# Eight units in the first routing group, and two sigmoid groups in another place

## The chip, the core and the metric

One core of a Trainium2 chip. The metric is the device time of one execution in microseconds; the figure for a kernel is the median of its runs.

## What is computed

Two stages, the second on the output of the first. Stage one is a gated linear attention with a running state (batch 4, 8 heads, 768 steps, head size 40), stage two a mixture of eight experts with two experts per token (3072 tokens of 320 features, hidden size 1024).

```python
for t in range(S):                       # attention
    m_new = np.maximum(f_gate[:, :, t] + m, i_gate[:, :, t])
    f_stab = np.exp(f_gate[:, :, t] + m - m_new); i_stab = np.exp(i_gate[:, :, t] - m_new)
    C = f_stab * C + i_stab * outer(vt, kt);  n = f_stab * n + i_stab * kt
    denom = np.maximum(np.abs(n . qt), 1.0)
    y[:, :, t] = sigmoid(o_gate[:, :, t]) * (C @ qt) / denom

logits = x @ w_gate                      # routing
noisy = logits + np.log1p(np.exp(x @ w_noise)) * noise
top2 = the two largest of noisy;  top2_w = softmax over these two
for e in range(8):                       # experts
    h = np.maximum(x[tokens of e] @ w1[e], 0.0)
    out[tokens of e] += top2_w * (h @ w2[e])
```

## The kernel before

**Attention loop.** The recurrence is worked in chunks of 64 steps. A unit is one chunk of one pair of batches, 128 tokens; there are 24 units. The loop `while i < NU - LEAD` runs iterations 0 to 21, one per unit; units 22 and 23 are written out behind it. The order of instructions on each engine is written by hand: the program text is the order of each engine's queue. Iteration i works on several units at once: DVE scales the keys of unit i+1 (`k_part`, L367), PE updates the state (`c_part`, L387) and ACT copies it into the next unit's operand (L390); PE forms the outputs of unit i (`o_part`, L396); `e_part` makes the decays of unit i+2 in two halves, each a PE matmul (L336) into one PSUM bank and an ACT exponential out of it (L339); DVE normalizes (`f_part`, L401 to L407) and POOL multiplies by the sigmoid of the output gate (L408); DVE multiplies scores by decays for unit i+1 (`p_part`, L373, or L377 in halves); PE makes router logits of unit i-2 (`l_part`, L439), transposes the rows of unit i-1 (`t_part`, L419) and makes scores of unit i+2 (`s_part`, L359). Loads of unit i+3 are issued by SP and POOL at the top of the iteration (`load_unit`), where POOL or SP also stores finished rows to DRAM (`keep_rows`).

**Sigmoids.** ScalarE keeps one table set with exponential and logarithm; a sigmoid is three ACT steps in place (`sig_part`, L345): exponential of -x, logarithm of one plus that, exponential of its negative. The steps of unit i+1 stand in iteration i, the first ahead of `o_part`, the other two at its end; iterations 0 and 1 differ.

**Routing.** Six groups of four units (`GROUPS`). When the logits of a group's last unit are there, a generator `g_part(g)` is put into a list, and `fill` deals out its small DVE steps: up to 0.2 (in the program's own units of about a microsecond, 0.19 for most steps) behind `k_part`, 0.15 twice within `f_part`, and the rest of 1.6 at the iteration's end. The generator makes the noisy logits (three ACT steps are asked for in between, L719), the two largest and their indices (L569, L572), the weights (L575, L602 to L605), a running count of tokens per expert (rank matmuls `r_part`, L448 to L450), and from each token's rank one-hot tables OA (L649, L652) and OB (L655), steps marked "long", which only the fill at the iteration's end takes. A burst (`b_part`, L459) multiplies the tables of four units and adds to TBL, the list of tokens per expert and place; `done` counts the units in it. Tables are double buffered.

**What waits for the table.** Expert 0's rows are gathered (POOL, indirect DMA, L803) in three parts: when 12 units are done (`begun`, at the top of an iteration, two tiles, a third in the next), when 20 are done, and when all are. Behind the loop PE transposes the gathered rows (L833) and begins with expert 0 (`mm1`, L1031). The second part is gathered in the stretch of 72 matmuls that finish the first part of expert 0 (L1154); its transposes stand in the last third of these. There `advance` deals out the remaining routing. From then on the experts follow one another, with PE's order fixed throughout. POOL also makes the low parts of the first expert's weights, one piece (L147) at the end of iterations 11, 13, 17, 19, 20 and 21.

Of the kernel before, what the change touches and what calls it, by code (L numbers as in the profile page):

```python
# [10 lines left out]
HF = mybir.dt.float16  # L11
# [3 lines left out]
OP = mybir.AluOpType  # L15
# [3 lines left out]
NE, F, DM = 8, 1024, 320  # L19
# [8 lines left out]
TC = BLK // 128  # L28
# [5 lines left out]
FIT = 2048  # L34
FF = 1024
NM = 768
GROUPS = tuple((u, 4) for u in range(0, 24, 4))
GOF = {u: g for g, (u0, n) in enumerate(GROUPS) for u in range(u0, u0 + n)}
NB = 4

EF, LONG = 2, 3
NR = NE - EF
# [25 lines left out]
def build(ctx, tc, qk, vk, og, fi, noise, wgn, w1, w2, cst, ce, out):  # L68
    nc = tc.nc
    V, A, P, T, SP = nc.vector, nc.scalar, nc.gpsimd, nc.tensor, nc.sync  # L70
# [14 lines left out]
    spot = keep.tile([128, 128, 2], HF, name="spot")  # L85
    cols = keep.tile([128, NE * TC, 2], HF, name="cols")
    sgn = keep.tile([128, 2 * NU], HF, name="sgn")
# [47 lines left out]
    def piece_w1(j):  # L135
        k, p = j // 2, j % 2 if j < 4 else 1
        SP.dma_start(RAW1[64 * p:64 * p + 64, k], w1[0, 64 * j:64 * j + 64])
# [203 lines left out]
    def sig_part(u, ps_=(0, 1, 2)):  # L341

        g = SG[u % 4]
        for p in ps_:
            A.activation(g, g, (AF.Exp, AF.Ln, AF.Exp)[p], bias=float(p == 1), scale=(-1.0, 1.0, -1.0)[p])  # L345
# [64 lines left out]
    def keep_rows(u):  # L410
        (P if u < XV - 1 else SP).dma_start(XD[128 * u:128 * u + 128, 0:DM], XR[u])
# [86 lines left out]
    def decode(a, b, more=True):  # L498
        run(decode_steps(a, b, more))
# [10 lines left out]
    def lc_part(i, t, w):  # L510
        u = i - 2
        if 0 <= u < NU:
            g = GOF[u]
            c = u - GROUPS[g][0]
            if c == 0:
                LG[g] = rt.tile([128, NB, 16], F32, name="lg")
            A.activation(LG[g][:, c, :], t[:, LGC:LGC + 16], AF.Copy)
# [6 lines left out]
    anew = {}  # L524
    for nb in sorted({n for _, n in GROUPS}):
        anew[nb] = rt.tile([128, NE, nb + 1], BF, name=f"anew_{nb}", bufs=1)
        P.memset(anew[nb], 1.0)
        P.memset(anew[nb][:, :, 0], 0.0)
    bursts, done, acts, lag = [], [0], [], [1, 1]
    OBT = [rt.tile([128, 4, 128, 2], HF, name=f"ob{i}", bufs=1) for i in range(2)]  # L530
    OAT = [rt.tile([128, 4, NE * TC, 2], HF, name=f"oa{i}", bufs=1) for i in range(2)]

    def g_part(g):

        u0, nb = GROUPS[g]
        lg = LG[g][:, 0:nb]
        f = lambda a: a.rearrange("p u e -> p (u e)")
        fe = lambda a: a.rearrange("p e u -> p (e u)")
        sm = lambda name, shape, dt=F32: rt.tile(shape, dt, name=f"{name}_{nb}", bufs=1)
# [93 lines left out]
        ai = sm("ai", [128, 2 * nb], I32)  # L633
        V.tensor_scalar(ai, f(r), 7, None, op0=OP.arith_shift_right)
        yield
        n = 2 * nb
        assert n == 8
        bi = sm("bi", [128, n], HF)
        V.scalar_tensor_tensor(bi, ai, -128.0, f(r), op0=OP.mult, op1=OP.add)
        yield  # L640
        ah = sm("ah", [128, n], HF)
        V.tensor_copy(ah, ai)
        while done[0] < u0 - 4:
            yield "wait"
        OB, OA = OBT[g % 2], OAT[g % 2]
        C = NE * TC
        yield "long"
        two = lambda a, c: a.rearrange("p (a b) -> p a b", b=2)[:, :, None, :].to_broadcast([128, 4, c, 2])
        V.tensor_tensor(OA, cols[:, None].to_broadcast([128, 4, C, 2]), two(ah, C), op=OP.is_equal)  # L649
        yield 0.3  # L650
        yield "long"
        V.tensor_mul(OA, OA, two(sgn[:, 2 * u0:2 * u0 + n], C))  # L652
        yield 0.3
        yield "long"
        V.tensor_tensor(OB, spot[:, None].to_broadcast([128, 4, 128, 2]), two(bi, 128), op=OP.is_equal)  # L655
        yield 0.6
        bursts.append(([OB[:, j // 2, :, j % 2] for j in range(n)], [OA[:, j // 2, :, j % 2] for j in range(n)], unit[0] + lag[1]))
        if u0 + nb == NU:
            V.tensor_add(rk[:, 0:1], rk[:, 0:1], bump[0])
            yield  # L660
# [37 lines left out]
    spent, long = [0.0], set()  # L698
# [48 lines left out]
    def route(i):  # L747
        if 2 <= i <= NU + 1 and sum(GROUPS[GOF[i - 2]]) == i - 1:
            routing.append(g_part(GOF[i - 2]))
# [91 lines left out]
    unit = [0]  # L841
    clear = zeros()
    pre1 = first_w1()
    i = 0
    while i < NU - LEAD:
        unit[0] = i
        spent[0] = 0.0
        if 1 <= i and i + 3 < NU:
            load_unit(i + 3, "kv")
        if i:  # L850
            keep_rows(i - 1)
        if 1 <= i and i + 3 < NU:
            load_unit(i + 3, "g")
        if i % 2 == 0 and i and i // 2 + 2 < 2 * GB:
            gate_move(i // 2 + 2, (P, P) if i < XV else (SP, SP))

        if i in W1LD:
            piece_w1(W1LD.index(i))
        if i == W2AT:
            early_w2(0, 4)  # L860
        if i == 4:
            SP.dma_start(cs[:, C_TRI:], cst[:, C_TRI:])
        if i == 5:
            SP.dma_start(nzt, noise)
        while sent:
            SP.dma_start(*sent.pop())
        if not begun and done[0] >= E0U[0]:
            decode(0, E0S[1] // 128, 128 * E0U[0] > FIT)
            begun = 1
        if begun and late < len(tiles(0, 0)):  # L870
            gather(0, 0, tiles(0, 0)[late:late + 2])
            late += 2
            begun = 2
        if i == 6:
            constants()
            A.activation(tri, cs[:, C_TRI:C_TRI + 128], AF.Copy)
            A.activation(ones, cs[:, C_ONE:C_ONE + 128], AF.Copy)
            A.activation(sgn, cs[:, C_SGN:C_SGN + 2 * NU], AF.Copy)
        if i in (6, 7):
            n = slice(64 * (i - 6), 64 * (i - 6) + 64)  # L880
            A.activation(spot[:, n], cs[:, C_N:C_N + 128][:, n, None].to_broadcast([128, 64, 2]), AF.Copy)
        if i == 7:
            A.activation(cols, cs[:, C_COL:C_COL + NE * TC, None].to_broadcast([128, NE * TC, 2]), AF.Copy)
        asked = len(acts)
        k_part(i + 1)
        fill(0.2, False)
        s_room(i + 2)
        c_part(i)
        if i:
            sig_part(i + 1, (0,))  # L890
        o_room(i)
        o_part(i)
        e_part(i + LEAD, (0,))
        act(asked)
        if i == 0:
            sig_part(0)
        f_part(i, lambda: fill(0.15, False))
        p_part(i + 1)
        t = l_part(i)
        w = r_part(t)  # L900
        b = None if w else b_part(t)
        if i:
            t_part(i - 1)
            tc_part(i - 1)
        lc_part(i, t, w)
        bc_part(t, b)
        if i < 2:
            s_part(i + 2)
            e_part(i + LEAD, (1,))
            sig_part(i + 1, (1, 2) if i else (0, 1, 2))  # L910
        else:
            e_part(i + LEAD, (1,))
            s_part(i + 2)
            act()
            sig_part(i + 1, (1, 2))
        route(i)
        fill((SHARE if i < NU - 3 else 0.6) - spent[0])
        if i in W1AT:
            next(pre1)
        if i < 6:  # L920
            gates_on(GATES[i + 1])
        if 6 <= i < 13:
            P.memset(XG[:, i - 6], 0.0)
        i += 1
# [8 lines left out]
    u = NU - 2  # L933
# [19 lines left out]
    u = NU - 1  # L953
# [197 lines left out]
    for k, (l, r) in enumerate(((HH, W2H), (HLO, W2H), (HH, W2L))):  # L1151
        for n in range(24):
            t, j = divmod(n, 8)
# [261 lines left out]
```

## Time and profile before

| | us |
|---|---|
| median of three runs | 514.81 |
| lowest and highest run | 512.7, 516.75 |
| span of the profiled execution | 512.4 |
| PE busy in it | 497.5 (97%) |
| DVE, ACT, POOL busy | 331.3, 245.7, 231.1 |

The time of the profiled execution is given by its span, from the first instruction to the last; the runs' times are those of other executions. In the rows further down, times are microseconds from the span's start. PE is the matmul engine, PEld its weight loads, DVE the vector engine, ACT the scalar engine, POOL GpSimd, and SPq the queue of SyncE. L373 is line 373 of the kernel before. A bracket at the end of a timeline row is the engine's idle time ahead of the instruction and what ended it.

### The profile page before, as it was taken

What the parts mean: (1) busy time and instruction counts of PE and PEld (TensorE: products, weight loads), DVE (VectorE), ACT (ScalarE), POOL (GpSimd) and SP (SyncE); (2) the same over time, 40 slices, a digit from 0 to 9 for tenths busy, and PEclk for the clock granted to TensorE, in tenths of its full rate; (3) what the DMA queues carried; (4) which work ended last, traced back from release to release, by engine and by line L of the source; (5) the groups of instructions that cost most, each with busy time, mean ns of one, the idle gap of its engine ahead of it and who ended that gap; (6) DMA issues with size and microseconds to landing.
All of it is one profiled execution on the core that took longest, in us unless ns stands there. A gap on an engine that the chain in (4) does not pass through costs nothing.

```text
span 512.4 us, 13150 instructions
## 1 busy us (share of the span) xinstructions
PE 497.5 (97%) x5043; PEld 472.3 (92%) x5043; DVE 331.3 (65%) x935; ACT 245.7 (48%) x584; POOL 231.1 (45%) x303
## 2 busy tenths in 40 slices
PE   8899999998999999999999999999999999999995
PEld 4698888887999988999999999999999999999994
DVE  8868889889787586754853675375448347555410
ACT  7768888898623355423531543154235315514300
POOL 9736666265113876156135605531561354151033
PEclk9969999999999999999999999999999999999998
DMA  6888787877767465296159417723941682372033
GB/s 168 237 224 259 211 245 207 228 209 230 260 217 234 108 98 180 46 242 157 30 100 271 104 28 195 171 79 68 278 90 39 162 203 80 65 169 26 2 36 45
DMA packets 51493, 76.89 MB, mean 150 GB/s; under 512 B 10825, under 2 KB 41808, under 8 KB 51392
## 3 DMA queue, kind: packets, MB, share of 16 engines
q1 hardware_dynamic: 38576, 50.16, 33.7%
q0 software_dynamic: 12848, 25.82, 24.0%
q8 instruction: 42, 0.69, 0.6%
q14 instruction: 27, 0.22, 0.1%
HBM read 52.10 MB, written 17.32 MB: 135 GB/s over the span
## 4 chain that ended last, share of the span: by engine, by line
PE 83%; DVE 8%; DMA 4%; ACT 2%; issue 1%; POOL 1%; SPq 1%; POOLq 0%; DVEq 0%
PE s L1031 25%; PE e L1031 12%; PE o L1066 5%; PE o L1065 5%; PE o L1064 5%; PE st L1066 5%; PE st L1065 5%; PE st L1064 5%; PE o L396 3%; DVE p L373 2%; PE e L336 2%; PE s L359 1%; PE s L1154 1%; PE xt L439 1%; PE st L387 1%; DVE kd L367 1%
## 5 line engine op out<-in xcount | busy, mean ns | idle before, releaser
L1087 POOL DMA_INDIRECT y_out<-y,tok x53 | 87.2, 1646 | 178.6 <-DVE y L1077 177.5
L1044 ACT ACTIVATE hx<-s 128x384 fp32r<-128x384 f32 (+5 forms) x91 | 43.5, 478 | 72.7 <-PE s L1031 67.9
L1031 PE MATMUL s<-xh,w1h 128*128 128x384 f32 (+6 forms) x273 | 76.0, 336 | 0.0
L803 POOL DMA_INDIRECT xg<-rows,tok x53 | 56.3, 1062 | 35.7 <-issue 13.7
L1047 DVE SCALAR_TENSOR_TENSOR hx<-s,hx 128x384 fp32r<-128x384 f32 (+3 forms) x91 | 48.1, 528 | 34.2 <-ACT hx L1044 34.0
L1031 PE MATMUL s<-xh,w1l 128*128 128x384 f32 (+6 forms) x273 | 61.9, 334 | 0.0
L1066 PE MATMUL o<-w2h,hx 128*128 128x320 f32 x184 | 56.9, 309 | 0.0
L1064 PE MATMUL o<-w2h,hx 128*128 128x320 f32 x184 | 56.8, 309 | 0.0
L1065 PE MATMUL o<-w2l,hx 128*128 128x320 f32 x184 | 56.8, 309 | 0.0
L1066 PE MATMUL st<-w2h,hx 128*128 128x320 f32 x176 | 54.4, 309 | 0.0
L1064 PE MATMUL st<-w2h,hx 128*128 128x320 f32 x176 | 54.4, 309 | 0.0
L1065 PE MATMUL st<-w2l,hx 128*128 128x320 f32 x176 | 54.3, 309 | 0.0
L1031 PEld LDWEIGHTS s<-xh,w1h 128*128 128x128 f32 x273 | 48.8, 188 | 1.3 <-ACT xh L835 0.3
L1031 PEld LDWEIGHTS s<-xh,w1l 128*128 128x128 f32 x273 | 47.8, 188 | 1.1 <-DVE xh L837 0.2
L1031 PE MATMUL s<-xl,w1h 128*128 128x384 f32 (+6 forms) x182 | 46.0, 334 | 0.0
L1044 ACT ACTIVATE hx<-e 128x384 fp32r<-128x384 f32 (+5 forms) x45 | 21.7, 482 | 48.9 <-PE e L1031 36.2
L1077 DVE TENSOR_SCALAR y<-o,gw 128x320 f32<-128x320 f32 x23 | 12.7, 550 | 45.8 <-PE o L1066 45.8
L1077 DVE TENSOR_SCALAR y<-st,gw 128x320 f32<-128x320 f32 x22 | 12.1, 551 | 43.3 <-PE st L1066 43.3
L1031 PE MATMUL e<-xh,w1h 128*128 128x384 f32 (+6 forms) x135 | 38.4, 338 | 0.0
L408 POOL TENSOR_TENSOR xr<-tm,vk 128x320 f32<-128x320 f32 x24 | 20.9, 871 | 35.3 <-ACT w L339 10.4
L345 ACT ACTIVATE vk<-vk 128x320 f32<-128x320 f32 x72 | 33.8, 471 | 2.8 <-DMA vk<-og_in 1.9
L1064 PEld LDWEIGHTS o<-w2h,hx 128*128 128x128 f32 x184 | 34.5, 188 | 0.0
(247 smaller groups left out, 1242.1 us busy)
## 6 DMA issues: line engine op xcount, KB each, us to landing
raw<-w_in SPq DMA_DIRECT2D x6, 1280.0 KB, 6.9
qk<-qk_in SPq DMA_DIRECT2D x24, 256.0 KB, 3.9
raw<-w_in SPq DMA_DIRECT2D x6, 1024.0 KB
y_out<-zrow SPq DMA_DIRECT2D x15, 320.0 KB, 4.2
raw<-w_in SPq DMA_DIRECT2D x17, 256.0 KB, 7.7
vk<-vk_in POOLq DMA_DIRECT2D x24, 162.0 KB, 3.9
vk<-vk_in SPq DMA_DIRECT2D x24, 162.0 KB, 4.0
vk<-og_in SPq DMA_DIRECT2D x24, 160.0 KB, 3.6
```

The costliest lines, as they stand in the source:

```text
L345: A.activation(g, g, (AF.Exp, AF.Ln, AF.Exp)[p], bias=float(p == 1), scale=(-1.0, 1.0, -1.0)[p])
L396: T.matmul(OQ[u][half[p], h, :], PP[u][n, p, h, :], VK[u % 4][p][n, h * 41:h * 41 + 41], start=True, stop=True)
L408: P.tensor_mul(XR[u], tm.rearrange("p h d -> p (h d)"), SG[u % 4])
L803: P.indirect_dma_start(out=XG[0:rows_of(e, t), t], out_offset=None, in_=XD[0:n], in_offset=bass.IndirectOffsetOnAxis(ap=token(e, t), axis= ...
L1031: T.matmul(ps[:, 0:n], l, r, start=i == 0, stop=i == len(ops) - 1)
L1044: A.activation(hi, x, AF.Relu)
L1047: V.scalar_tensor_tensor(lo, top[0], 0.0, top[1].bitcast(F32), op0=OP.max, op1=OP.subtract)
L1064: T.matmul(ps, HH[:, j, c], W2H[:, j], start=j == 0, stop=False)
L1065: T.matmul(ps, HH[:, j, c], W2L[:, j], start=False, stop=False)
L1066: T.matmul(ps, HLO[:, j, c], W2H[:, j], start=False, stop=j == 7)
L1077: V.tensor_scalar(y[0:n], ps[0:n], GW[e][0:n, t:t + 1], None, op0=OP.mult)
L1087: st = P.indirect_dma_start(out=out, out_offset=bass.IndirectOffsetOnAxis(ap=token(e, t), axis=0), in_=y[0:n], in_offset=None, compute_op= ...
```

## The change

Two edits. The first two routing groups become one of eight units: `GROUPS` begins with (0, 8), the logit tile holds eight units, and in `g_part` the part that makes one-hot tables runs once for each four units of a group, waiting each time until the tables in that buffer are used. The group of eight enters the list when the logits of unit 7 are there, at the end of iteration 9, where the second group entered before; the groups behind it keep their units. The other edit moves sigmoids: those of unit 1 from the end of iteration 0 to iteration 1, behind the first half of the decays, and the first step of unit 2 from the front of iteration 1 to its end, where the other two stand.

```diff
-GROUPS = tuple((u, 4) for u in range(0, 24, 4))
+GROUPS = ((0, 8), (8, 4), (12, 4), (16, 4), (20, 4))
...
-NB = 4
+NB = 8
...
-        n = 2 * nb
-        assert n == 8
-        bi = sm("bi", [128, n], HF)
+        bi = sm("bi", [128, 2 * nb], HF)
         V.scalar_tensor_tensor(bi, ai, -128.0, f(r), op0=OP.mult, op1=OP.add)
         yield
-        ah = sm("ah", [128, n], HF)
+        ah = sm("ah", [128, 2 * nb], HF)
         V.tensor_copy(ah, ai)
-        while done[0] < u0 - 4:
-            yield "wait"
-        OB, OA = OBT[g % 2], OAT[g % 2]
-        C = NE * TC
-        yield "long"
+        C, n = NE * TC, 8
         two = lambda a, c: a.rearrange("p (a b) -> p a b", b=2)[:, :, None, :].to_broadcast([128, 4, c, 2])
-        V.tensor_tensor(OA, cols[:, None].to_broadcast([128, 4, C, 2]), two(ah, C), op=OP.is_equal)
...
+        for uh in range(u0, u0 + nb, 4):
+            while done[0] < uh - 4:
+                yield "wait"
+            OB, OA = OBT[uh // 4 % 2], OAT[uh // 4 % 2]
+            own_ = slice(2 * (uh - u0), 2 * (uh - u0) + n)
+            yield "long"
+            V.tensor_tensor(OA, cols[:, None].to_broadcast([128, 4, C, 2]), two(ah[:, own_], C), op=OP.is_equal)
+            yield 0.3
+            yield "long"
+            V.tensor_mul(OA, OA, two(sgn[:, 2 * uh:2 * uh + n], C))
+            yield 0.3
+            yield "long"
+            V.tensor_tensor(OB, spot[:, None].to_broadcast([128, 4, 128, 2]), two(bi[:, own_], 128), op=OP.is_equal)
+            yield 0.6
+            bursts.append((...))
...
         c_part(i)
-        if i:
+        if i > 1:
             sig_part(i + 1, (0,))
         o_room(i)
         o_part(i)
         e_part(i + LEAD, (0,))
         act(asked)
-        if i == 0:
-            sig_part(0)
+        if i < 2:
+            sig_part(i)
...
         if i < 2:
             s_part(i + 2)
             e_part(i + LEAD, (1,))
-            sig_part(i + 1, (1, 2) if i else (0, 1, 2))
+            if i:
+                sig_part(i + 1)
```

## Rows read from the trace of the kernel before

**Rows 1.** The page: tenths of TensorE's full clock, forty slices

```profile
PEclk9969999999999999999999999999999999999998
```

**Rows 2.** Windows: PE, PEld, DVE, ACT, POOL busy; clock, DMA share, GB/s

```profile
24.00:25.00 1.00, 1.00 (x21) 0.69 (x22) 0.22 (x1) 0.57 (x2) 0.08 (x1) 0.50 0.94 325
33.00:34.00 1.00, 1.00 (x35) 1.00 (x31) 0.00 (x0) 0.39 (x1) 0.00 (x0) 0.65 0.94 293
```

**Rows 3.** Timeline from 19 us: start, us, engine, line, operation, wait

```profile
19.27 1.46 ACT L345 ACTIVATE vk<-vk 128x320 f32<-128x320 f32 x3
20.76 0.90 ACT L390 ACTIVATE vk<-st 40x328 f32<-40x328 f32 x2
22.59 0.47 ACT L345 ACTIVATE vk<-vk 128x320 f32<-128x320 f32 x1 [0.93 <-DMA vk<-og_in]
22.96 0.58 ACT L339 ACTIVATE w<-e 128x512 f32<-128x512 f32 x1
...
23.59 0.79 PE L336 MATMUL e<-re,le 98*128 98x512 f32 x1 [2.00 <-ACT w L339]
```

**Rows 4.** Timeline of DVE: the product of iterations 1, 3, 5, 9 and 21

```profile
21.66 1.22 DVE L373 TENSOR_TENSOR p<-s,w 128x1024 f32<-128x1024 f32 x1
...
35.61 1.22 DVE L373 TENSOR_TENSOR p<-s,w 128x1024 f32<-128x1024 f32 x1
...
44.42 1.22 DVE L373 TENSOR_TENSOR p<-s,w 128x1024 f32<-128x1024 f32 x1
...
64.27 1.22 DVE L373 TENSOR_TENSOR p<-s,w 128x1024 f32<-128x1024 f32 x1
...
123.78 1.22 DVE L373 TENSOR_TENSOR p<-s,w 128x1024 f32<-128x1024 f32 x1
```

**Rows 5.** Timeline of DVE, from the product of iteration 14 to that of 15

```profile
88.68 1.21 DVE L373 TENSOR_TENSOR p<-s,w 128x1024 f32<-128x1024 f32 x1
89.81 0.23 DVE L555 TENSOR_TENSOR co<-co,na 128x32 f32<-128x32 f32 x1
...
91.26 0.81 DVE L367 TENSOR_TENSOR kd<-vk,w 128x640 f32<-128x640 f32 x1
...
93.10 1.22 DVE L373 TENSOR_TENSOR p<-s,w 128x1024 f32<-128x1024 f32 x1
```

**Rows 6.** Groups of DVE instructions by line, 60 to 126 us: busy, mean

```profile
L655 DVE TENSOR_TENSOR ob<-spot,bi 128x1024 f16<-128x1024 f16 x4 | 2.7, 682 | 0.0
...
L649 DVE TENSOR_TENSOR oa<-cols,ah 128x448 f16<-128x448 f16 x4 | 1.6, 392 | 0.1
```

**Rows 7.** Timelines of DVE and POOL: a wait, a long instruction

```profile
49.63 0.19 DVE L551 SCALAR_TENSOR_TENSOR co<-t,ue 128x32 f32<-128x32 f32 x1 [1.52 <-ACT t L719]
...
113.44 2.25 DVE L575 TENSOR_TENSOR d<-mx 128x4 f32<-128x4 f32 x1
...
114.39 1.27 POOL L147 TENSOR_TENSOR w1l<-raw,w1h 128x512 fp32r<-128x512 f32 x1
```

**Rows 8.** Chain that ended last, POOL's timeline, landing: the second gather

```profile
146.51 1.17 PE e L1154 x8
...
148.28 0.23 PE o L459 x8
...
153.72 0.33 PE s L833 x3
...
150.00 1.03 POOL L803 DMA_INDIRECT xg<-rows,tok  x1 [10.12 <-DVE km L490]
...
xg<-rows,tok POOLq DMA_INDIRECT x1, 3.1
```

**Rows 9.** Timelines of POOL and PE, landing: first gather, third tile

```profile
116.51 1.61 POOL L803 DMA_INDIRECT xg<-rows,tok  x1 [0.31 <-issue]
...
126.91 0.49 PE L833 MATMUL st<-cs,xg 128*128 128x128 f32 x3
...
xg<-rows,tok POOLq DMA_INDIRECT x1, 5.2
```

More of the change, by code (lines that the diff above doesn't have):

```diff
@@ L635, in g_part @@
         yield
-        n = 2 * nb
-        assert n == 8
-        bi = sm("bi", [128, n], HF)
+        bi = sm("bi", [128, 2 * nb], HF)
         V.scalar_tensor_tensor(bi, ai, -128.0, f(r), op0=OP.mult, op1=OP.add)
         yield
-        ah = sm("ah", [128, n], HF)
+        ah = sm("ah", [128, 2 * nb], HF)
         V.tensor_copy(ah, ai)
-        while done[0] < u0 - 4:
-            yield "wait"
-        OB, OA = OBT[g % 2], OAT[g % 2]
-        C = NE * TC
-        yield "long"
-        two = lambda a, c: a.rearrange("p (a b) -> p a b", b=2)[:, :, None, :].to_broadcast([128, 4, c, 2])
-        V.tensor_tensor(OA, cols[:, None].to_broadcast([128, 4, C, 2]), two(ah, C), op=OP.is_equal)
[L650 to L657, printed above, removed]
+        C, n = NE * TC, 8
+        two = lambda a, c: a.rearrange("p (a b) -> p a b", b=2)[:, :, None, :].to_broadcast([128, 4, c, 2])
+        for uh in range(u0, u0 + nb, 4):
[12 more added lines that the diff above has]
+            yield 0.6
+            bursts.append(([OB[:, j // 2, :, j % 2] for j in range(n)], [OA[:, j // 2, :, j % 2] for j in range(n)], unit[0] + lag[1]))
         if u0 + nb == NU:
```

## The prediction

> **What bounds the kernel now.** I read the page first: PE is nearly always busy, with one dent in its granted clock, in the third slice, 25.6 to 38.4 us [rows 1]. So a gain has to be PE time: a place where PE waits, or one where it runs slowly. The one-microsecond windows show the slow place: the clock is at its half level (1.2 GHz) at 24 us and up to about 33.7, since the window 33 to 34 has a mean of 0.65 [rows 2]: some 9.7 us at half rate. Just ahead of it the timeline has PE idle for 2.00 us at L336, waiting for ACT [rows 3]. Follow that backwards: PE's second decay matmul of unit 3 needs the PSUM bank that ACT's exponential empties at 22.96; ACT came to that exponential late because the sigmoid step in front of it (22.59) had waited 0.93 us for the output gates of unit 2; and the state copies before that (20.76) had stood behind three sigmoid steps of unit 1 (19.27) [rows 3].
>
> Next I took the starts of the product L373, one per loop iteration, as a clock of the loop [rows 4]. Iterations 4 and 5, with no routing, take (44.42-35.61)/2 = 4.405 us each: the pace that PE sets. Iterations 2 and 3 together take 35.61-21.66 = 13.95 us, 5.14 more than two such. Iterations 6 to 9 (routing of units 0 to 3) take 19.85, 2.23 over four; iterations 10 to 21 take 59.51, 6.65 over twelve. Where there is routing, DVE sets the pace: iteration 15 has 1.13 for the product, 1.45 of routing steps until L367 and 1.84 from there to the next product, 4.42 in all [rows 5]. So a period is about 2.75 us, plus what routing puts between the product and L367, plus what little it puts just behind L367; PE's 4.405 hides about 1.6 us of routing.
>
> **The sigmoids.** Nothing is removed; three ACT steps of unit 1 go from the end of iteration 0 to the middle of iteration 1, and one of unit 2 from the front of iteration 1 to its end. They issue no DMA. With the three gone, ACT does the copies of iteration 1 at about 19.3 instead of 20.76 and the next exponential at about 20.2 instead of 22.96, so PE never meets the gap of 2.00. The moved steps follow: unit 1's three (1.46) and one exponential later, unit 2's come at about 22.9, after 22.59, when its gates were there, so the DMA wait is gone too. Late next is ACT: six sigmoid steps in a row of work push the copies of iteration 2 some 1.3 us behind PE's matmuls. I put 0.3 of that on PE (an estimate; the rest lies beside PE's own work of that iteration). SP issues the loads one after another here, no faster than before, and they move data nearly all the time (DMA share 0.94 [rows 2]), so I take another 0.4 off: 5.14 - 0.3 - 0.4, **-4.4**. Bounds: -2.0 if only the gap goes and the clock falls all the same, -5.14 if both periods become 4.405.
>
> **The routing.** What goes is one pass of the small steps: some twenty DVE instructions, four ACT, one POOL product, three rank matmuls and one store of weights. What stays is everything per unit: maxima, indices, one-hot tables, bursts. The eight-unit instructions have twice the columns. The order in which steps are dealt out follows from the budgets in fill; I worked it through by hand.
>
> Iterations 6 to 9 have no routing left. Iteration 6 loses the 1.52 us in which DVE stood at L551 for ACT's logarithm chain [rows 7], queued ahead of the reciprocals and products; ACT's constants of that iteration stay, and I leave 0.1 for them. All four come to PE's pace: **-2.1** (bounds: -0.7, if the constants hold DVE for the same 1.52, and -2.23).
>
> Iterations 10 to 21, in order: 10 still waits for the logarithm chain, with wider operands, 5.0; 11 has three more maxima, 4.5; 12 has eight index searches between product and L367, 4.9; 13 only two small steps, PE's pace, 4.4. Iteration 14 takes the rank product and its five small successors (about 0.2 to 0.3 each), two table steps of 0.39 and one of 0.68 for units 0 to 3 [rows 6], some 2.4 us between product and L367, and a stall (below): 5.8. Iteration 15 has the same three table steps for units 4 to 7 and begins the next group, 4.6; 16 and 17 take 4.4 and 4.6; 18 to 21 take 4.65, 4.75, 5.8 and 4.7, since the group of units 12 to 15 no longer ends inside the loop. The sum is 58.1 against 59.51: **-1.4**. Bounds: -3.3, half of all the excess there, and +2.2, the whole of what iterations 6 to 9 cost before, paid a second time.
>
> The stall is seen in the row of d: 2.25 us for four columns, over when POOL's L147 is over [rows 7]. L147 (1.27 us) stands at the end of iterations 11, 13, 17, 19, 20 and 21. At 11 DVE now does index searches beside it; at 13 it meets the table steps, and I count 0.55 of a possible 1.27 there. The Trainium skill (GPSIMD Engine Reference, Specifications) says that GpSimd and VectorE share SBUF interfaces and contend for DVE instructions in a two-port mode or with two SBUF inputs. By that rule all table steps beside L147 pay, which is rival B.
>
> **The gathers behind it.** Work has moved later. The bursts of units 0 to 3 and 4 to 7 go from iterations 10 and 14 to 15 and 16, that of units 8 to 11 from 18 to 19. So the gather of expert 0's first two tiles starts at iteration 20 instead of 19, and the third tile's at 21. Before, the third started on POOL at 116.51 and landed 5.2 later, at 121.7; PE wanted it at 126.91 [rows 9]. One iteration later this margin of 5.2 is about used up: **+0.2** (0 to 1.6, the latter with L147 in front of it on POOL).
>
> The burst of units 16 to 19 comes behind the 42nd L1154 matmul instead of the 28th. Eight of them take 1.17, so it is 14 x 0.146 = 2.05 us later. Before, it ended at 148.51, POOL's gather began at 150.00 and landed 3.1 later, at 153.1; PE's transposes stand at 153.72 [rows 8]. So 0.6 was spare, and PE, which has nothing else in its order, now waits: 2.05 - 0.6, **+1.45** (0 to 2.05). The second tile follows behind five more matmuls and adds nothing.
>
> **Sum**: -4.4 - 2.1 - 1.4 + 0.2 + 1.45 = -6.25 against the profiled span of 512.4, so 506.15. That execution is near the fastest of the three runs (512.7); against their median it is 514.81 - 6.25 = 508.56, and I forecast **508.5**.
>
> **Rivals** (times against the median).
> A. The clock falls at the start all the same, or the loads come late. For it: the windows' DMA share. Against it: what is left of PE's idle time there is in pieces under 1 us. The start then gives 2.0, the sum is -3.85: 511.
> B. The merged group is dear: stalls beside L147 make iterations 10 to 21 give +1.0 instead of -1.4. For it: the row of 2.25; against it: fewer two-input steps than before. Sum -3.85: 511.
> C. The other side: PE's wait for the second gather lets the clock fall, in a stretch that PE alone bounds. The price is half the time at the low level: with the start's 9.7 us, 4.85, it is 513.4; from 12.5 us on it ends slower than before; with twice the 9.7 it is 518.3; slower by over 1% takes 23 us. For it: a wait of 2.00 was followed by the low level once; against it: 1.45 is shorter, and the page shows no second dent, whatever short waits the loop had.
> D. All near the good bounds: start -5.1, iterations 6 to 9 -2.2, iterations 10 to 21 -3.0, gathers +0.9: -9.4, 505.4.
>
> **How the numbers follow.** Forecast 0.48 (its own range 506 to 511), A 0.16, B 0.14, C 0.13, D 0.09. For 8 in 10 I take 504.5 to 513: it holds forecast, A, B and D and leaves out most of C and the edges of the others. One per cent, about what a measurement of this kernel can tell from no change, is 5.15 us, so faster means under 509.66: most of the forecast (0.44), D (0.09) and a little of A and B (0.04), 0.57. Slower is the far end of C, 0.04. Within 1% is the rest, 0.39.
>
> **What would show it.** Right: no half-level window between 22 and 34 us; the exponential of unit 3 at about 20 instead of 22.96; products L373 4.4 apart in iterations 4 to 9; that of iteration 21 about 8 us before 123.78; PE idle for 1 to 2 us ahead of L833 in the L1154 stretch. Wrong: a clock of 0.5 near 25 us, or again behind the L1154 stretch; iterations 11 to 15 above 5 us each; L833 without a wait, which would mean that the gather had more room than I gave it; PE waiting behind the loop for the first three tiles.

## The result and the profile after

The changed kernel takes 517.64 us (median of 14 runs, 515.45 to 525.89), the kernel before 514.06 beside it (14 runs). The ratio is 1.0072, 95% interval 1.0054 to 1.0089: slower by 0.7%, where 1.2% faster was forecast. (A ratio here leaves out executions that are over 1.5% above the fastest of their kernel measured with them.) The profiled span is 517.8 against 512.4. A run's time is its span plus 1.8 us here (519.57 for the span of 517.8), so the profiled execution of before stood at 514.2, its median, and not near the fastest; that of after is 2 us above its median.

The clock of the page has three dents instead of the two of [rows 1]: a smaller one at the start, one in the ninth and tenth slices, and the end.

```profile
PEclk9989999988999999999999999999999999999998
```

The product L373 of iterations 1, 3, 5, 9, 10 and 21 in the timeline of DVE after, against [rows 4]:

```profile
21.68 1.22 DVE L373 TENSOR_TENSOR p<-s,w 128x1024 f32<-128x1024 f32 x1
32.64 1.22 DVE L373 TENSOR_TENSOR p<-s,w 128x1024 f32<-128x1024 f32 x1
41.79 1.22 DVE L373 TENSOR_TENSOR p<-s,w 128x1024 f32<-128x1024 f32 x1
63.39 1.22 DVE L373 TENSOR_TENSOR p<-s,w 128x1024 f32<-128x1024 f32 x1
69.35 1.21 DVE L373 TENSOR_TENSOR p<-s,w 128x1024 f32<-128x1024 f32 x1
124.81 1.22 DVE L373 TENSOR_TENSOR p<-s,w 128x1024 f32<-128x1024 f32 x1
```

At iteration 3 the kernel is 3.0 us ahead, at 5 2.6, at 9 0.9, and at 10 nothing is left (69.04 before). The table cuts five profiled executions into stages by starts of instructions: the products p of iterations 3, 9, 10, 21 and of unit 23 ("tail"), the first matmul of expert 0, the first L1154 (L1155 after) and the first matmul behind it. "Low clock" is the time at half level (1.2 GHz) up to there.

| us | before | after | e3 | e5 | e7 | forecast, after - before |
|---|---|---|---|---|---|---|
| start to p3 | 35.61 | 32.64 | 30.72 | 32.87 | 32.86 | -4.4 (to p5) |
| p3 to p9 | 28.66 | 30.75 | 30.58 | 27.02 | 27.71 | -2.1 |
| p9 to p10 | 4.77 | 5.96 | 6.81 | 6.52 | 6.83 | +0.23 |
| p10 to p21 | 54.74 | 55.46 | 53.95 | 52.96 | 55.30 | -1.6 |
| p21 to tail | 1.73 | 3.15 | 3.15 | 2.67 | 2.47 | 0 |
| tail to first expert matmul | 4.81 | 5.83 | 6.59 | 9.38 | 5.65 | +0.2 |
| first part of expert 0 | 13.51 | 13.41 | 13.43 | 14.36 | 13.42 | 0 |
| the 72 matmuls of L1154 | 12.04 | 13.46 | 12.28 | 13.50 | 12.29 | +1.45 |
| rest | 356.53 | 357.14 | 357.29 | 357.02 | 357.37 | 0 |
| low clock ahead of the rest | 10.2 | 10.2 | 0 | 10.2 | 3.4 | |

The differences before to after add up to +5.4: -2.97, +2.09, +1.19, +0.72, +1.42, +1.02, -0.10, +1.42, +0.61. Two of them are not what they look like. The start holds 10.2 us of low clock before and 3.4 after; half of the difference, 3.4 us (an estimate of what it cost), is more than the 2.97 that the start gained. And "p21 to tail" is work that changed its place: iteration 21 took 3.45 us where it took 5.74 before, since the table steps of that group are no longer in it, and the product of the tail then waited for PE's scores; from the product of iteration 20 to the tail it is 6.60 against 7.47. The tail's product after, in DVE's timeline:

```profile
127.96 1.23 DVE L373 TENSOR_TENSOR p<-s,w 128x1024 f32<-128x1024 f32 x1 [0.54 <-PE s L359]
```

What eats the lead between 32 and 69 us are waits of PE that the kernel before had not: PE's timeline after, where "issue" means that no semaphore of the trace released it.

```profile
44.11 0.97 PE L359 MATMUL s<-qk 64*64 64x64 f32 x25 [0.68 <-issue]
51.32 0.56 PE L359 MATMUL s<-qk 64*64 64x64 f32 x11 [1.93 <-issue]
```

They stand in the middle of a row of 32 like matmuls, 7 and 21 into it. The page has a DMA queue of another kind than the data queues, 42 packets of 16 KB; PE has 10,080 recorded instructions (5040 matmuls, 5040 weight loads), 240 for each packet:

```profile
q8 instruction: 42, 0.69, 0.6%
```

So the theory to be tested: PE stands still because the next block of its own program comes late among the data loads (the "loads theory"); its rivals were the merged group itself, the gathers, and the clock.

### The profile page after: what moved, and what is told of

It reads as the page before. It is cut to its first block, busy times and chain, and to the rows that moved or that the text cites. A ratio compares the mean times of both kernels' runs of the same rounds, so it can differ in the third digit from the quotient of the medians.

```text
span 517.8 us, 13112 instructions
## 1 busy us (share of the span) xinstructions
PE 498.0 (96%) x5040; PEld 472.1 (91%) x5040; DVE 329.3 (64%) x915; ACT 244.9 (47%) x579; POOL 229.8 (44%) x304
## 4 chain that ended last, share of the span: by engine, by line
PE 85%; DMA 3%; POOL 3%; DVE 3%; ACT 2%; issue 2%; SPq 0%; POOLq 0%; DVEq 0%
PE s L1032 24%; PE e L1032 12%; PE o L1067 5%; PE o L1066 5%; PE o L1065 5%; PE st L1067 5%; PE st L1066 5%; PE st L1065 5%; PE o L396 3%; PE s L359 3%; PE e L336 2%; PE st L387 2%; PE xt L439 2%; PE xt L419 1%; DMA xg<-rows,tok 1%
## 5 line engine op out<-in xcount | busy, mean ns | idle before, releaser
L803 POOL DMA_INDIRECT xg<-rows,tok x53 | 55.1, 1040 | 35.2 <-issue 14.3
L359 PEld LDWEIGHTS s<-qk 64*64 64x64 f32 x768 | 26.2, 142 | 12.2 <-issue 7.7
```

Source lines behind the costliest of these rows:

```text
L359: T.matmul(SQ[u][:, p][half[p], h, :], q[r, 1, h, :], q[r, 0, h, :], start=True, stop=True)
L803: P.indirect_dma_start(out=XG[0:rows_of(e, t), t], out_offset=None, in_=XD[0:n], in_offset=bass.IndirectOffsetOnAxis(ap=token(e, t), axis= ...
```

## The experiments

**One edit at a time.** e1 is the kernel before with the second edit, e2 the changed kernel with it undone.

```diff
-        if i:
+        if i > 1:
             sig_part(i + 1, (0,))
...
-        if i == 0:
-            sig_part(0)
+        if i < 2:
+            sig_part(i)
...
-            sig_part(i + 1, (1, 2) if i else (0, 1, 2))
+            if i:
+                sig_part(i + 1)
```

(e1; in e2 the same lines the other way.)

> The kernel before with the sigmoids' new order alone, routing groups of four as before. If the sigmoids' order gains at the start and the merged group loses it (the routing theory): start 3 us earlier at the product of iteration 3 (32.6), iterations 6 to 9 as before (19.9), second gather without a wait, 511 us in all, ratio 0.994. If the gain at the start is lost in the loads whatever the routing does (the loads theory, PE standing still for 0.7 and 1.9 us without a semaphore in iterations 5 and 6 when it runs ahead): the product of iteration 9 stands within 0.7 of the 64.27 of before, and the time is 513.5 to 514.5, ratio 1.00.

> The changed kernel with the sigmoids where they were: the merged group alone. By the prediction's steps: iterations 6 to 9 2.1 less, 10 to 21 1.4 less, gathers 1.65 more, 512.3. By the routing theory (the group is dear in iterations 10 to 21 and at both gathers): iterations 6 to 9 at PE's pace, 17.7 instead of 19.85, then 2 to 3 lost in 10 to 21, 0.9 at the third tile and 1.45 at the second gather: 516.5. By the loads theory PE shows no standstill in iterations 5 to 8 here, since it comes there 3 us later.

Measured: e1 513.97 against 513.9, ratio 0.9992 (0.9962 to 1.0021); e2 518.76, ratio 1.0092 (1.0060 to 1.0125). The sigmoids' order is worth nothing that these runs can tell, and the group costs all of the loss. The profiled executions of the two (521.05 and 526.49) were the longest of their runs, so their stages show which waits there are and not what an edit costs. e1 has p3 at 32.76 and p10 at 72.38, later than before, with the standstills of after at the same two instructions (0.41 and 2.20) and 6.8 us of low clock behind the second. In e2 p3 stands at 32.42, although the sigmoids are in their old order: the 35.61 of [rows 4] is not what that order must give. e2 has standstills too, 1.32 in iteration 4 and 1.10 in iteration 10, against its expectation of none.

**The loads.** e4 moves three loads out of iterations 4 to 6, e5 moves all that the later routing allows behind iteration 9, e6 adds three.

```diff
-W1LD, W1AT, W2AT = (6, 9, 12, 15, 18), (11, 13, 17, 19, 20, 21), 21
+W1LD, W1AT, W2AT = (9, 10, 12, 15, 18), (11, 13, 17, 19, 20, 21), 21
...
-        if i == 4:
+        if i == 7:
             SP.dma_start(cs[:, C_TRI:], cst[:, C_TRI:])
-        if i == 5:
+        if i == 8:
             SP.dma_start(nzt, noise)
```

That is e4; e5 has 10 and 9 for the 7 and the 8, `W1LD = (11, 12, 14, 15, 18)` and `W1AT = (15, 16, 17, 19, 20, 21)`; e6 is the changed kernel with

```diff
+        if i in (4, 5, 7):
+            piece_w1({4: 1, 5: 4, 7: 1}[i])
```

> The changed kernel with three loads that nothing wants yet moved out of iterations 4 to 6: the constants from 4 to 7 (with their ACT copies from 6 and 7 to 9 and 10), the noise from 5 to 8, the first piece of the first expert's weights from 6 to 9 (the second from 9 to 10): 640 KB. By the loads theory PE no longer stands still in iterations 5 and 6, the product of iteration 9 comes 2.5 to 4 us earlier than 63.39, and the total is 513.5 to 515. If the standstills have nothing to do with what the DMA engines carry, they stay at their places and the total stays at 517.6.

> The changed kernel with everything that its later routing allows moved behind iteration 9: noise from 5 to 9, constants from 4 to 10 (their ACT copies from 6 and 7 to 12 and 13), the first two weight pieces from 6 and 9 to 11 and 12 (with their L147 from 11 and 13 to 15 and 16), the third from 12 to 14. Until the product of iteration 10 that is 0.9 MB less to move. If PE's standstills between 30 and 70 us come from what the DMA engines carry (loads theory): none over 0.3 us in iterations 4 to 9, the product of iteration 10 at 64 to 66 instead of 69.35, and most of that is kept, 513.5 to 515. If the loads have to be paid wherever they stand (as the moved ones were in iteration 9 of the run before this one), standstills of 1 to 3 us come in iterations 10 to 15 and the total stays at 517 to 519.

> The changed kernel with three more loads of 256 KB each at iterations 4, 5 and 7 (pieces of the first expert's weights, loaded again later in their place, so the result is the same). Loads theory: at some 245 GB/s 768 KB are 3.1 us, and since PE has no slack against the loads, the product of iteration 10 comes 2 to 3.1 us later than in the changed kernel (69.35), with longer standstills. If DMA has room, it stays within 0.7 of 69.35.

Measured: in e4 p3 to p9 is 26.73, in e5 27.02: six periods of 4.405 are 26.43, so the standstills there are gone but for one of 0.39 in e5, and iterations 6 to 9 come to PE's pace as the prediction had it. In e4 the bill comes in iteration 10 (9.45 us), where the moved loads now are. The windows show where the DMA engines are full (columns as in [rows 2], the DMA share ahead of the GB/s), of after and of e4, and PE's timeline in e4 the new standstill:

```profile
42.00:46.00 4.00, 3.32 (x84) 2.23 (x83) 2.98 (x6) 2.74 (x10) 2.94 (x5) 1.00 1.06 269
46.00:50.00 4.00, 3.39 (x62) 2.74 (x59) 2.73 (x5) 3.49 (x10) 4.00 (x10) 1.00 0.99 259
```

```profile
42.00:46.00 4.00, 4.00 (x107) 3.65 (x108) 3.76 (x10) 3.31 (x9) 1.94 (x3) 1.00 0.91 258
50.00:54.00 4.00, 4.00 (x104) 3.60 (x101) 3.57 (x6) 3.48 (x9) 3.61 (x8) 1.00 0.67 141
62.00:66.00 4.00, 1.82 (x68) 1.64 (x60) 0.21 (x2) 2.77 (x8) 2.87 (x6) 0.98 1.03 270
```

```profile
65.65 1.81 PE L396 MATMUL o<-vk,p 128*64 128x41 f32 x30 [2.18 <-issue]
```

A share of 1.06 and 0.99 with standstills, 0.91 and 0.67 without, 1.03 with one again.

In e5 p10 stands at 66.41 instead of 69.35 and the lead lasts to the tail (122.04 against 127.96). In e6 p10 stands at 73.84, 4.5 later than after, and PE waits longest just behind the last added load:

```profile
58.48 1.19 PE L387 MATMUL st<-vk,kd 104*40 104x41 f32 x28 [2.60 <-issue]
```

More bytes, later; fewer bytes, PE's pace: the loads theory holds from 32 to 70 us. In the total it does not show: e4 1.0220 (1.0167 to 1.0273) and e5 1.0078 (1.0049 to 1.0108), both expected at 513.5 to 515, took 523.77 and 518.11; e6 is one run of 524.56. What e5's profiled execution had won it lost at the first gather, whose third tile PE waited for, with the low clock behind it (6.8 us of it): timeline of PE, then the windows (columns as in [rows 2]).

```profile
125.84 0.52 PE L833 MATMUL st<-cs,xg 128*128 128x128 f32 x3 [1.58 <-DMA xg<-rows,tok]
```

```profile
126.00:127.00 1.00, 1.00 (x10) 1.00 (x10) 0.66 (x3) 0.49 (x1) 1.00 (x1) 0.83 0.76 105
127.00:128.00 1.00, 1.00 (x10) 0.67 (x10) 0.64 (x2) 0.17 (x1) 0.92 (x2) 0.50 0.93 308
```

**Whose blocks.** e8 puts 112 more instructions ahead of everything on PE.

```diff
-WARM, WARM2, WARM3 = 16, 5, 2
+WARM, WARM2, WARM3 = 8, 5, 2
...
+        for _ in range(64 if n == WARM else 0):
+            T.matmul(wp[:, 0:8], wz[:, 0:128], wz[:, 0:8], start=True, stop=True)
```

> The changed kernel with 8 of the 16 first warm-up matmuls of PE replaced by 64 tiny ones: 112 instructions more ahead of everything else on PE, at about the same time. PE's standstills between 30 and 55 us stood at the same instructions in three executions (7 matmuls into s_part of unit 7, 21 into that of unit 8, 14 further on; one iteration is some 228 instructions of PE, 256 a block of 16 KB). If PE waits for blocks of its own instructions: the standstills come at other instructions, 56 matmuls ahead of the old places (within c_part or o_part of the iteration before, or e_part), and none at the old ones. If it waits for data of s_part that the trace doesn't name: they stay at L359, at the same matmuls.

Measured (one run, 521.4): the standstill is no longer at L359 but one matmul before the end of the 32 of L387, about the 56 matmuls ahead; none stands at the old places.

```profile
39.91 0.23 PE L387 MATMUL st<-vk,kd 128*40 128x41 f32 x1 [1.70 <-issue]
```

In e3, whose loop is that of the changed kernel, the standstill of 0.68 came back at the old place with the old length (25 matmuls from the end of L359); the one of 1.93 did not, and another stood at L387, where e6 has its longest (27 and 28 from the end):

```profile
42.66 0.97 PE L359 MATMUL s<-qk 64*64 64x64 f32 x25 [0.68 <-issue]
...
53.55 0.70 PE L387 MATMUL st<-vk,kd 104*40 104x41 f32 x27 [0.69 <-issue]
```

So the place belongs to PE's instruction stream and not to the data of L359. The trace settles it, since it has every packet of the instruction queue: PE goes on just behind one. After, the DMA view of 41.5 to 41.6 us and that of 48.6 to 48.7 us hold one packet each, begun at 41.53 and 48.67; the last figure is its time as a share of 16 engines' 0.1 us, so they took 1.20 and 1.19 us.

```profile
q8 instruction: 1, 0.02, 75.3%
q8 instruction: 1, 0.02, 74.5%
```

They ended at 42.73 and 49.86, and PE went on at 44.11 and 51.32, 1.38 and 1.46 us later. It is so at 41 standstills of 0.4 to 2.6 us in fourteen of the seventeen profiles (none in before, e11 and e12): PE goes on 1.2 to 1.7 us behind the end of a packet. Counted in PE's recorded matmuls they stand at 595, 721, 846, 972, 1098, 1224 and so on, 125 or 126 apart, in e8 at 722 with 56 matmuls more ahead. Up to 120 us, in the other sixteen profiles, each packet began between 0.7 us ahead and 5.2 us behind PE's crossing of the boundary before (median 3.6 behind where a standstill followed, 1.9 elsewhere): the stream is about one block ahead, and a packet that starts late leaves PE nothing to do. That other loads make it late rests on e4, e5 and e6.

The Trainium skill (Runtime: NRT & Kernel Launch, Instruction fetch mechanics) says that the sequencer fetches the program in blocks of 16 KiB, 256 instructions, by a DMA queue of its own, and that crossing a block costs one tail-bump of that queue, mostly hidden. The traces agree with the blocks (125 or 126 matmuls with as many weight loads) and disagree on the cost: 0.4 to 2.6 us at the 41 standstills, with a DMA share of 0.44 to 1.07 over the four us ahead, 0.85 or more in 29 of them.

**The gathers.** e3 puts the burst of units 16 to 19 back in its place, e7 gathers the third tile with the other two as well.

```diff
-    lag[:] = 10, 9
+    lag[:] = 10, 2
```

(e3 and e7)

```diff
-            gather(0, 0, tiles(0, 0)[late:late + 2])
-            late += 2
+            gather(0, 0, tiles(0, 0))
+            late += 3
```

(e7)

> The changed kernel, with the burst of units 16 to 19 due in the place where it stood before (lag 2 instead of 9). If the 1.43 us at the second gather are the burst's place alone: L833 of that gather waits under 0.3 instead of 1.24, 1.0 to 1.4 less in all, 516.4. If the wait only moves (to the table steps on DVE, or to POOL), under 0.5 less. Its attention loop is instruction by instruction that of the changed kernel, so it also shows whether PE's standstills of 0.68 and 1.93 us in iterations 5 and 6 come back in another execution.

> The changed kernel with both gathers' waits taken away by earlier issue: all three tiles of the first gather in iteration 20 instead of two there and one at 21 (so the third is no longer queued behind L147 on POOL), and the burst of units 16 to 19 in its old place. If the waits there are the cost: from the product of the tail to the first matmul of expert 0 5.0 instead of 6.1 to 7.4 us, the sums 12.1 to 12.3 instead of 13.5, 2 to 2.5 us in all, 515.3. If the third tile's lateness comes from ACT's copies of the weights in front of L835, the first of these stays above 5.8.

After, the third tile's gather was queued on POOL behind L147, and the second gather's rows came late (timelines of POOL and PE):

```profile
124.32 1.27 POOL L147 TENSOR_TENSOR w1l<-raw,w1h 64x512 fp32r<-64x512 f32 x1 [1.75 <-ACT w1h L146]
125.86 1.02 POOL L803 DMA_INDIRECT xg<-rows,tok  x1 [0.27 <-POOL w1l L147]
...
155.23 1.03 POOL L803 DMA_INDIRECT xg<-rows,tok  x1 [10.04 <-DVE mx L569]
...
158.24 0.55 PE L833 MATMUL s<-cs,xg 128*128 128x128 f32 x3 [1.24 <-DMA xg<-rows,tok]
```

In e3 the stretch of L1155 takes 12.28 instead of 13.46; what is left of the wait is for the table on DVE, ahead of the burst:

```profile
149.75 0.39 PE L459 MATMUL o<-oa,ob 128*128 128x56 f16 x8 [0.16 <-DVE ob L655]
...
155.19 0.49 PE L833 MATMUL s<-cs,xg 128*128 128x128 f32 x3
```

In e7 it is 12.29, so the second wait is the gather's lateness. From the tail to the first expert matmul e7 has 5.65, where executions with the late tile have 5.83 (after) to 10.12 (e2). There the gather is only part of it: PE waited 1.58 to 1.97 us for the third tile in e2, e4, e5 and e8, but after it landed 0.2 us before PE came to it, and e1, with groups of four and an early gather, has 6.06. The totals are inside the scatter: e3 519.88 in four runs (1.0128, 1.0083 to 1.0173) with one of 516.63; e7 516.95, ratio 1.0064 (1.0035 to 1.0094), the profiled execution 515.66.

**Both repairs, with either order of the sigmoids, and groups of four beside them.** e9 and e12 have e5's loads, e7's gathers and the piece L147 of iteration 17 moved to 19; e12 has the old order of the sigmoids. e10 and e14 (the same kernel) are the kernel before with the new order and the first two weight pieces loaded at 11 and 12; e11 is that without the new order. e13 has e5's loads and e7's gathers only; e15 is the changed kernel. So the rows "loads moved" below hold fewer moved loads on the left, and the early gathers on the right.

```diff
-W1LD, W1AT, W2AT = (6, 9, 12, 15, 18), (11, 13, 17, 19, 20, 21), 21
+W1LD, W1AT, W2AT = (11, 12, 13, 15, 18), (14, 15, 17, 19, 20, 21), 21
```

(e10, e11, e14; in e9 and e12 `W1AT = (15, 16, 19, 19, 20, 21)` on top of e5 and e7)

> The changed kernel with the three repairs together: loads behind iteration 9 as in e5_loads_past_ten, both gathers issued early as in e7_gathers_early, and of the L147 pieces the one at 17 moved to 19 (two there), away from the table steps of iteration 17. If the losses found so far are all of it: product of iteration 10 at 66 or 67, iterations 17 and 18 0.9 less, tail to first matmul of expert 0 5 to 5.7 and sums 12.3, so a span of 510 to 511.5 and a ratio of 0.993 to 0.997. If PE's waits only move on, 513.5 to 515, ratio 1.000 or above.

> Routing groups of four as before, the sigmoids' new order, and the first two weight pieces loaded at 11 and 12 instead of 6 and 9 (the third at 13; their L147 at 14 and 15). With the sigmoids alone the product of iteration 10 stood at 72.4. Loads theory: with 0.5 MB less to move by then PE comes through iterations 3 to 9 without a standstill over 1 us, the product of iteration 10 stands at 66 to 68, and 1.5 to 3 us of it are kept: 511 to 512.5, ratio 0.994 to 0.997. If the sigmoids' order itself is worth nothing: as in the next run, within 0.5 us.

> The kernel before with only the weight pieces moved as in e10_sigmoids_relieved. Before had no standstill of PE over 0.3 us in iterations 3 to 9, because its start was late. So nothing to gain there: 513 to 514.5, ratio 0.998 to 1.002. It is also another look at the start of the old order: if the half-level stretch of 10.2 us behind the ACT wait of 2.0 us is the rule there, the product of iteration 3 stands at 35 to 36; if it was chance, at 32 to 33.5.

> As e9_group_relieved with the sigmoids in their old order. What the sigmoids' order is worth once loads, gathers and L147 are out of the way is the difference to e9_group_relieved: by the prediction's step 3 to 4 us, by the start measured so far (product of iteration 3 at 32.4 in the group alone against 30.7 to 32.9 with the new order) under 1.5.

> The changed kernel with the loads behind iteration 9 (as in e5_loads_past_ten) and both gathers issued early (as in e7_gathers_early), nothing else. If the losses are the loads and the gathers: product of iteration 10 at 66 to 67, tail to the first matmul of expert 0 5 to 5.7, sums 12.3, ratio 0.996 to 1.000, and 1% under the changed kernel beside it. If what is left of the group (waits for p in iterations 10, 14, 17, 18 and 20) and the clock behind them cost 0.9% as in every pair so far: 1.003 to 1.006.

> The kernel of e10_sigmoids_relieved once more: groups of four, the sigmoids' new order, the first two weight pieces loaded at 11 and 12. If the 0.9967 there was a gain: 0.994 to 0.998. If it was scatter: 0.999 to 1.002, as the sigmoids alone.

> The changed kernel itself, beside the two: 1.006 to 1.009 as on the first chip. In its trace PE's standstills come back at the same instructions (7 matmuls into L359 of iteration 5, 21 into that of iteration 6), with other lengths.

| ratio to the kernel before | groups of four | first eight as one group |
|---|---|---|
| old order | 1 | e2 1.0092 (1.0060 to 1.0125) |
| new order | e1 0.9992 (0.9962 to 1.0021) | after 1.0072 (1.0054 to 1.0089), e15 1.0159 (1.0069 to 1.0249) |
| old order, loads moved | e11 1.0011 (0.9966 to 1.0055) | e12 1.0100 (1.0059 to 1.0142) |
| new order, loads moved | e10 0.9967 (0.9908 to 1.0027), e14 1.0039 (0.9998 to 1.0079) | e9 1.0052 (1.0016 to 1.0089), e13 1.0099 (1.0042 to 1.0156) |

Measured beside each other, the kernels with the group are 0.6 to 0.9% above those without (e2 against before, e12 against e11, e9 against e10, e13 against e14; the last pair's intervals overlap). The order of the sigmoids gains nothing that these runs can tell, with the loads moved or not, and no repair brings the group back to the kernel before. e15 keeps two executions, and its interval and e13's overlap, so what the two repairs give back in the total is not shown; e13, e14 and e15 all lie above what was expected of them. In e9, e12 and e13 PE has no standstill at a block boundary left between 30 and 69 us (p3 to p9 26.43 to 26.75). In e9, from the product of iteration 19 to the tail it took 16.0 us against 11.7 in e5, with small DVE steps at 1.31 and 1.19 us beside the two pieces of L147 and short waits of PE beside the three gathers; which of them cost the time is open. No version beat both kernels.

The last seven runs were on chips on which the kernel before takes 524.5 us. All seven profiles there show PE waiting 2.5 us near 175 us for ACT, which itself had been standing; none of the earlier ones does, and the low clock followed in five. PE's timeline in e9:

```profile
177.28 0.57 PE L1033 MATMUL e<-xh,w1h 128*128 128x160 f32 x2 [2.56 <-ACT xh L835]
```

What ACT waited for there stays open; the kernels with either grouping had it.

## Why the prediction was wrong, step by step

**The two edits apart.** The sigmoids were put at -4.4 us and gave -0.4 (e1, interval -2.0 to +1.1). The group was put at -2.1 - 1.4 + 0.2 + 1.45 = -1.85 and cost +4.7 (e2, +3.1 to +6.4). Both terms failed, each for its own reason.

**The sigmoids, -4.4.** The mechanism was right in part: the gap of 2.00 [rows 3] is gone. But ACT was late one iteration on: in six of the thirteen profiles with the new order PE waits 1.14 us at L336 near 28.4, where the sum had 0.3 for it. The term failed twice. First, its size was the 9.7 us of low clock in one execution [rows 2]. Of the four profiles with the old order two have such a stretch (p3 at 35.61 and 36.50) and two have little or none (32.42, 32.37; the latter, e12, with the gap at 2.42); the thirteen with the new order have p3 from 30.7 to 35.1, 32.65 on average, against 34.2: 1.6 us. The 35.05 is e9, with 10.2 us of low clock: the new order doesn't prevent it. With no low clock at the start p3 is 32.37 in the old order (e12) and 30.71 to 31.72 in the new (e3, e14, e15); with 3.4 us it is 32.42 (e2) and 32.64 to 32.87. Second, no lead here lasts. The sentence that took 0.4 off for loads "no faster than before" was the step to follow to its end: with a DMA share of 0.94 [rows 2] a PE that is ahead meets its loads, its own program among them. That is rival A, priced at 2.4 for the start alone; it took all of it.

**Iterations 6 to 9, -2.1.** They took 21.60 instead of 19.85: +1.75. Without the two standstills and what the second held up they are at PE's pace, and with the loads gone they were measured there (e5: p5 to p9 18.21, against 17.6). So the routing's part was right, and the bound that came next, the arrival of PE's own instruction blocks, had no term in the sum.

**Iterations 10 to 21, -1.4.** They took 61.42, +1.9. Iteration 10 took 5.96 to 6.28 instead of 5.0 where no standstill fell into it (after, e8, e9, e12, e13, e15): the wait for the logarithm chain is the one of [rows 7], but no late product ahead of it hides it now, and the reciprocal behind it has twice the columns (0.55):

```profile
68.33 0.23 DVE L551 SCALAR_TENSOR_TENSOR co<-t,ue 128x64 f32<-128x64 f32 x1 [1.25 <-ACT t L719]
68.54 0.55 DVE L553 RECIPROCAL na<-t 128x64 f32<-128x64 f32 x1
69.35 1.21 DVE L373 TENSOR_TENSOR p<-s,w 128x1024 f32<-128x1024 f32 x1
```

Iteration 14 took 6.70 instead of 5.8: a table step stood beside L147 on POOL and took 1.77 us, not 0.68 [rows 6]. In e5, where that L147 is elsewhere, it took 0.69, and the iteration 5.60. After, then e5:

```profile
85.81 1.31 POOL L147 TENSOR_TENSOR w1l<-raw,w1h 128x512 fp32r<-128x512 f32 x1 [2.08 <-ACT w1h L144]
85.89 1.77 DVE L655 TENSOR_TENSOR ob<-spot,bi 128x1024 f16<-128x1024 f16 x1
```

```profile
82.73 0.69 DVE L655 TENSOR_TENSOR ob<-spot,bi 128x1024 f16<-128x1024 f16 x1
```

Iterations 17 and 18 took 10.90 instead of 9.25, with L649 at 1.35 us beside L147 in place of 0.39; without that meeting they took 9.49 in e12, but 10.47 in e9, where PE was late too.

```profile
105.16 1.31 POOL L147 TENSOR_TENSOR w1l<-raw,w1h 128x512 fp32r<-128x512 f32 x1 [0.93 <-ACT w1h L144]
105.37 1.35 DVE L649 TENSOR_TENSOR oa<-cols,ah 128x448 f16<-128x448 f16 x1
```

That is rival B, with the rule of the Trainium skill quoted there (GPSIMD Engine Reference, Specifications): both rows agree with it, at 1.0 to 1.1 us a meeting, and I had counted 0.55 for one. Iterations 13, 16 and 21 were better than forecast (3.46 and 4.09 instead of 4.4 each, 3.45 instead of 4.7). The largest miss is iteration 20, 7.96 instead of 5.8: the low clock of 6.8 us from 112.4 on lies in it, and in e2 to e8, which have none there, it took 5.56 to 6.26.

**First gather, +0.2.** Queued behind L147 as the bound of 1.6 had it; from the tail to the first expert matmul +1.0 in the profiled execution, up to +2.6 in e4. After, 0.66 of it lies ahead of L833 and is in e1 too, and 0.3 ahead of the third tile, which had landed: neither is the gather's, so there its margin was used up and no more, as forecast. PE's waits for the tile in e2, e4, e5 and e8 are what the bound allowed for. **Second gather, +1.45.** +1.42: right, place and size, and undone by e3.

**The clock.** Rival C was right in kind and wrong in place: behind the second gather's 1.24 the clock held. Over all seventeen profiles, from 15 to 200 us, 20 of 25 waits of PE of 1.5 us or more were followed within 2 us by a stretch of 3.4 to 17 us at half level, 6 of 18 from 1.2 to 1.5, and 2 of 34 from 0.9 to 1.2. Seven of the 35 stretches came behind no such wait, both of after's (27.1 and 112.4 us) among them. The 1.93 at 51.32 after was spared; in e1 the wait at the same instruction was not (timeline, then windows), nor in e15 one of 1.94 ahead of the product of iteration 20:

```profile
51.09 0.56 PE L359 MATMUL s<-qk 64*64 64x64 f32 x11 [2.20 <-issue]
```

```profile
51.00:52.00 1.00, 0.91 (x31) 0.84 (x32) 1.00 (x7) 0.00 (x0) 0.01 (x1) 1.00 1.28 294
52.00:53.00 1.00, 1.00 (x34) 1.00 (x30) 0.09 (x1) 0.37 (x1) 0.00 (x0) 0.52 0.67 226
```

```profile
114.51 0.26 PE L396 MATMUL o<-vk,p 128*64 128x41 f32 x2 [1.94 <-issue]
```

```profile
116.00:117.00 1.00, 1.00 (x5) 0.77 (x5) 0.96 (x4) 0.11 (x1) 0.98 (x3) 0.50 0.62 172
```

The stretches come and go between executions: 10.2 us of low clock ahead of the rest before and after, none in e3, 27.3 in e2.

Single profiles don't give the average, but the record has the mean granted clock of every execution. One minus that, times the span, is the most that the half level can have cost (an estimate: half of the time spent at it, felt in full only where PE alone bounds). The changed kernel loses 4.7 us by it on average (clock 0.991). The kernel before loses 5.1 in the set beside e1 to e4 and 4.1 in that beside e5 to e8 (0.990 and 0.992; beside after it is not on record). So, as far as the record goes, the 0.7% is not clock but waits, and rival C did not come in the average. With the repairs it is the other way round: e9, e12 and e13 lose 14.7, 14.7 and 13.5, the kernel before beside them 9.6 and 9.1, and with that taken off they stand at 511.8, 511.8 and 511.5 us of span against 511.3 and 511.5. As far as this estimate goes, the repairs took the waits away, and the clock took the time back. Being an upper bound, it leaves room for some waits: among a kernel's own executions there the span grows by 0.55 to 0.73 us for each us of it. Why the kernels with the group were granted less clock there stays open. So does the +0.5 in the rest, which every kernel with the merged group has (357.0 to 357.5 against 356.5 and 356.6 on the first chips).

**The chances.** A, B and C were priced one at a time, and each at its price left a gain (511, 511, 513.4). A and B came together, A with a start worth nothing in the end, and iterations 6 to 9 lost on top, for which there was no rival; none of the four cases held that. The range ended at 513.0 for that reason.

## What to carry over

A wait that is removed gives time only until the next bound; where the DMA share is near 1, work out when the bytes of that stretch can be there before counting a lead. Before sizing a term by a low-clock stretch, ask whether another execution has it, and compare the mean clock of all executions before calling a difference clock or not. A step that is merged and moved meets other neighbours: write down what stands beside it on the shared engines in its new iteration, and price every meeting by the worst row seen.

## What the runs showed of the hardware

- PE stood still 0.4 to 2.6 us every so often at places 125 or 126 recorded matmuls apart in its program, and went on 1.2 to 1.7 us behind the end of a 16 KB packet of the instruction queue (41 standstills in 14 of 17 profiles); with 112 instructions put ahead the places moved by 56 matmuls.
- Two-input steps of DVE that began beside a two-input POOL instruction of 1.3 us: 1.77 instead of 0.69, 1.35 instead of 0.39. An L655 that was already running when L147 began kept 0.68 (five meetings), and the product L373, whose scores PE writes, kept 1.21 to 1.23 in 18 meetings.
- The longer PE had waited, the likelier a stretch at half level behind it: 2 of 34 waits of 0.9 to 1.2 us, 6 of 18 up to 1.5, 20 of 25 above; the same wait in the same kernel did or did not bring it.
